# One contraction a chunk from one tile of cosines and sines, waits of the gated unit by quarters, and a written-out sequence per engine

## The chip, the cores and the metric

The kernel runs on one core of one Trainium2 chip. The metric is the device time of one execution in microseconds (us), the median of several runs; less is better. The core has five queues that matter here: TensorE (PE, matrix products), VectorE (DVE), ScalarE (ACT), GpSimd (POOL), and SyncE (SP), which issues the DMA transfers. Each works through its own instructions in the order in which they were written, and an instruction that waits holds up all behind it on that engine.

## The reference

Two branches over a sequence of 2048 positions with 448 channels are mixed by a gate per position:

```python
x = A_u                                             # 1 x 2048 x 448
g = sigmoid((x * gate_w).sum(-1, keepdims=True))
# branch A: a state-space convolution, 256 complex states a channel
dt = exp(log_dt); A = -exp(log_A_real) + 1j * A_imag; C = (C_real + 1j * C_imag) * dt[:, None]
P = exp((A * dt[:, None])[:, :, None] * arange(2048)[None, None, :])
K = 2.0 * einsum("dn,dnl->dl", C, P).real           # a filter of 2048 taps a channel
y = irfft(rfft(u_t, 4096) * rfft(K, 4096))[:, :, :2048]   # causal convolution
a = transpose(y) + u * D_skip
# branch B: a gated linear unit, 448 -> 1792 -> 448
b = einsum("bsf,fd->bsd", sigmoid(x @ w_gate) * (x @ w_up), w_down)
return g * a + (1 - g) * b
```

## The kernel before

All products are made to float32 accuracy. For the large ones each factor is split into a rounded part and a remainder (`wh` and `wl`, `vh` and `vl`, `hh` and `hl` are such pairs; `xs` holds both parts of the input), and three products replace one.

There are four streams of work.

- **Prologue** (tiles of the pools `pre` and `pro`): the gate's dot products (`gt`, `dots`, which give the scales `gs` and `og`), then in two groups of channels the parameters of the filter. Its results go through DRAM as `phd` (phases) and `bsd` (decay steps).
- **Filter** (`kgen`, pools `eg` and `egp`): 28 chunks of 16 channels, each in two half-chunks of 128 states. POOL makes a table of decay powers `tb` from `bs` (one load serves two chunks). In `turns`, PE multiplies phases `ph` by positions into `tp` (L1128); ACT rounds that twice (L1138, L1139, into `fr` and `nn`); PE subtracts the rounded part (L1141); ACT takes the absolute value into `ec` (L1143) and the sine into `fr` (L1144), and turns `ec` into cosines (L1158). DVE multiplies tables into decays `es` (L1165, two products), forms the mirrored half (L1179, L1181), and multiplies `ec` and `fr` by the decays (L1183, L1185). PE contracts over the states into `kp` (L1191): 32 small products a half-chunk, in quarters of its array. ACT copies `kp` into `ke`, and after 14 chunks `ke` goes to DRAM as `kd`, one half of the channels.
- **Convolution** (`Chain`): a transform in two stages (L716, then L749) with a transposition between them, which for one half goes through the DRAM tensor `shf`. Spectra of the input are stored in DRAM as `us`. Later the filter's spectrum is made from `kd`, multiplied (L783), brought back (L793, L830) and added to the output. One large tile `fx_fu` holds in turn the input's first half, its second half, and the filter's first half; `fx_fk` takes the filter's second half in space that the filter's tiles leave.
- **Gated unit**: for each group of two or three blocks of 128 hidden channels, `glu_mm` (L1296 to L1301) gives `gu`, ACT and DVE form the hidden values (L1284 to L1288), `glu_down` (L1313 to L1315) gives `dn`, and L1322 or L1329 adds it to `ob`. Raw weights arrive in the tiles `xr` (five) and `vr` (one), and are split by L1270 and L1272.

The order of instructions is set before the program runs. Each operation is recorded with what it reads and writes and with a cost. `Plan.order` then plays the program through with a clock of those costs: it takes the engine that can start first, and on it the operation of the lowest rank among those that are ready. The table `RANK` gives ranks by engine, tile name and stage. Wherever such a clock lets a DMA's issue cost SP time, it is 450 ns.

Of the kernel before, what the change touches and what calls it, by code (L numbers as in the profile page):

```python
# [415 lines left out]
class Plan:  # L416
# [40 lines left out]
    def order(self):  # L457
# [5 lines left out]
        for key, x in RANK.items():  # L463
            x = x if isinstance(x, tuple) else (x,)
            for j, o in enumerate(kinds[key]):
                o["prio"] = x[j * len(x) // len(kinds[key])]
# [976 lines left out]
```

## Time and profile before

| | us |
|---|---|
| median of 3 runs (lowest to highest) | 741.96 (739.8 to 743.25) |
| the profiled execution, its own time | 740.59 |
| its span, first to last instruction | 738.8 |
| PE busy | 688.4 (93%) |
| DVE busy | 637.9 (86%) |
| ACT busy | 523.7 (71%) |
| POOL busy | 232.7 (32%) |
| mean granted clock of PE | 0.979 |

Busy time counts overlapped instructions once. A matrix product of 512 columns is shown for about 0.39 us though the next one starts 0.23 us after it, so a busy PE can hide lost time. The profile names a tile with its pool: `es_eg` is the tile `es` of the pool `eg`. What is late is read from the waits and from the stretches of time in which engines are less than full.

### The profile page before, as it was taken

Reading aid. Unit: us, or ns where it says so; the run is one execution under the profiler, and the core shown is the slowest. Engines: PE = TensorE matmul, PEld = TensorE weight load, DVE = VectorE, ACT = ScalarE, POOL = GpSimd, SP = SyncE. Lnnn points to the kernel's source line nnn. Section 1 sums busy time; section 2 is a strip of 40 time slices with the busy share of each in tenths; the row PEclk is TensorE's granted clock in tenths of the full one; section 3 lists DMA queues with packets and bytes.
Section 4 is the critical chain, followed back from the end, with each engine's and each line's share of the span. In section 5 each row is a group of like instructions: output and inputs, shape, how many; then the busy total and the mean of one; then the engine's idle time right before and its main releaser. Section 6 shows DMA issues by size and latency. Waiting matters only on the chain.

```text
span 738.8 us, 16536 instructions
## 1 busy us (share of the span) xinstructions
PE 688.4 (93%) x6628; PEld 498.6 (67%) x6628; DVE 637.9 (86%) x847; ACT 523.7 (71%) x962; POOL 232.7 (32%) x282
## 2 busy tenths in 40 slices
PE   4999899999999999978998899999999899999996
PEld 3788777677757776745666677777778566445863
DVE  6999998999999979999898779999995259775976
ACT  5578749999899779998998789999882342233110
POOL 0043446563455435434543324654400000000000
PEclk9999999999999999988999899999999999999998
DMA  9658337925949945469797913239516963787975
GB/s 291 200 122 217 108 79 203 239 91 171 202 121 223 219 107 160 171 175 204 183 232 180 220 45 125 86 133 175 119 40 131 271 226 100 249 304 207 168 191 142
DMA packets 98660, 126.12 MB, mean 171 GB/s; under 512 B 31224, under 2 KB 81080, under 8 KB 97560
## 3 DMA queue, kind: packets, MB, share of 16 engines
q1 hardware_dynamic: 98328, 124.61, 65.0%
q8 instruction: 52, 0.85, 0.5%
q0 software_dynamic: 256, 0.46, 0.3%
q14 instruction: 24, 0.20, 0.1%
HBM read 81.46 MB, written 43.58 MB: 169 GB/s over the span
## 4 chain that ended last, share of the span: by engine, by line
PE 42%; DVE 19%; ACT 16%; DMA 14%; issue 5%; SPq 3%; POOL 2%; ACTq 0%; DVEq 0%
PE kp_egp L1191 4%; PE gu_gps L1296 4%; PE dn_gps L1313 4%; PE gu_gps L1297 4%; PE gu_gps L1298 4%; PE dn_gps L1314 3%; PE dn_gps L1315 3%; DMA fx_fu<-shf 3%; SPq L615 3%; DVE es_eg L1165 2%; PE tp_egp L1128 2%; PE tp_egp L1141 2%; ACT nn_eg L1139 2%; DMA us<-fx_fu 2%; PE fps_fups L716 2%
## 5 line engine op out<-in xcount | busy, mean ns | idle before, releaser
L1296 PE MATMUL gu_gps<-xs_glu,wh_glu 128*128 128x512 f32 x336 | 138.1, 411 | 16.5 <-ACT wh_glu L1270 10.1
L1298 PE MATMUL gu_gps<-xs_glu,wl_glu 128*128 128x512 f32 x336 | 133.2, 397 | 0.4 <-DVE wl_glu L1272 0.4
L1297 PE MATMUL gu_gps<-xs_glu,wh_glu 128*128 128x512 f32 x336 | 133.3, 397 | 0.0
L1165 DVE TENSOR_TENSOR es_eg<-tb_eg 128x1024 f32<-128x1024 f32 x112 | 107.4, 988 | 7.0 <-POOL tb_eg L1115 3.7
L1313 PE MATMUL dn_gps<-vh_glu,hh_glu 128*128 128x448 f32 x224 | 87.9, 393 | 2.8 <-DVE ob_glu L1329 2.6
L1296 PEld LDWEIGHTS gu_gps<-xs_glu,wh_glu 128*128 128x128 f32 x336 | 64.1, 191 | 39.2 <-ACT wh_glu L1270 10.1
L1115 POOL TENSOR_TENSOR tb_eg<-tb_eg 128x96 f32<-128x96 f32 (+2 forms) x84 | 82.2, 982 | 6.2
L1314 PE MATMUL dn_gps<-vh_glu,hl_glu 128*128 128x448 f32 x224 | 82.6, 369 | 0.6 <-issue 0.4
L1315 PE MATMUL dn_gps<-vl_glu,hh_glu 128*128 128x448 f32 x224 | 82.3, 368 | 0.0
L1139 ACT ACTIVATE nn_eg<-fr_eg 128x512 fp32r<-128x512 f32 x112 | 75.0, 669 | 10.3 <-PE tp_egp L1141 10.1
L1329 DVE SCALAR_TENSOR_TENSOR ob_glu<-dn_gps,og,ob_glu 128x448 f32<-128x448 f32 x72 | 48.7, 677 | 30.2 <-PE dn_gps L1315 30.0
L1298 PEld LDWEIGHTS gu_gps<-xs_glu,wl_glu 128*128 128x128 f32 x336 | 64.0, 191 | 15.6 <-DVE wl_glu L1272 1.1
L1297 PEld LDWEIGHTS gu_gps<-xs_glu,wh_glu 128*128 128x128 f32 x336 | 64.2, 191 | 11.4
L1105 POOL MEMSET tb_eg<- 128x96 f32 x28 | 7.8, 283 | 201.1 <-DVE es_eg L1165 200.9
L1144 ACT ACTIVATE fr_eg<-tp_egp 128x512 f32<-128x512 f32 x112 | 69.9, 629 | 0.3 <-PE tp_egp L1141 0.3
L1185 DVE TENSOR_TENSOR es_eg<-fr_eg,es_eg 128x1024 f32<-128x1024 f32 x56 | 69.8, 1246 | 0.1
L1143 ACT ACTIVATE ec_eg<-tp_egp 128x512 f32<-128x512 f32 x112 | 69.4, 625 | 0.3 <-PE tp_egp L1141 0.2
L1183 DVE TENSOR_TENSOR ec_eg<-ec_eg,es_eg 128x1024 f32<-128x1024 f32 x56 | 69.5, 1241 | 0.1
L1138 ACT ACTIVATE fr_eg<-tp_egp 128x512 f32<-128x512 f32 x112 | 64.0, 636 | 7.2 <-DVE es_eg L1185 5.1
L1158 ACT ACTIVATE ec_eg<-ec_eg,half_pi 128x1024 f32<-128x1024 f32 x56 | 67.1, 1197 | 0.1
L1118 POOL TENSOR_TENSOR tb_eg<-tb_eg,bs_eg 128x32 f32<-128x32 f32 x84 | 62.0, 741 | 6.2
L1284 ACT ACTIVATE sg_glu<-gu_gps 128x512 f32<-128x512 f32 x56 | 34.0, 608 | 37.5 <-PE gu_gps L1301 35.3
(154 smaller groups left out, 1423.0 us busy)
## 6 DMA issues: line engine op xcount, KB each, us to landing
shf<-fx_fu SPq DMA_DIRECT2D x16, 896.0 KB, 4.1
fx_fu<-shf SPq DMA_DIRECT2D x16, 896.0 KB, 15.9
us<-fx_fu SPq DMA_DIRECT2D x16, 896.0 KB, 6.7
xr_glu<-in_w_dram SPq DMA_DIRECT2D x52, 256.0 KB, 3.0
ua_fk<-us SPq DMA_DIRECT2D x16, 448.0 KB, 6.0
uax_fk<-us SPq DMA_DIRECT2D x16, 448.0 KB, 4.5
vr_glu<-in_w_dram SPq DMA_DIRECT2D x28, 224.0 KB, 5.1
gt_pre<-in_u_dram SPq DMA_DIRECT2D x8, 448.0 KB, 4.9
```

What stands on the lines that cost most here:

```text
L1115: pool(96 * m, lambda n=n, m=m: G.tensor_mul(g3(n + 1, m), g3(1, m), g3(n, 1).to_broadcast([128, 32, 3, m])))
L1139: op("Act", c_act(512), lambda: S.activation(nn.real, fi(), AF.Copy, scale=-1.0, bias=MAGIC), [(fr, i)], [nn], prio)
L1144: op("Act", c_act(512, True), lambda: S.activation(fr[:, ds], tv(), AF.Sin, scale=TWO_PI), [tp], [(fr, i)], prio, table="sin")
L1165: V.tensor_mul(o.rearrange("p d (i k) -> p d i k", k=ny), x.unsqueeze(3).to_broadcast([128, 16, nx, ny]), y.unsqueeze(2).to_broadcast([128 ...
L1183: op("DVE", c_dve(1024), lambda: V.tensor_mul(ec[:, :, 32:96], ec[:, :, 32:96], es[:, :, 32:96]), [(es, 1), (es, 2)], [(ec, "p")], prio)
L1185: op("DVE", c_dve(1024), lambda: V.tensor_mul(es[:, :, 32:96], fr.real, es[:, :, 32:96]), [fr], [(es, 1), (es, 2)], prio)
L1296: T.matmul(p.real, wh[:, k, cs], x[:, k], start=(k == 0), stop=False)
L1297: T.matmul(p.real, wh[:, k, cs], x[:, 4 + k], start=False, stop=False)
L1298: T.matmul(p.real, wl[:, k, cs], x[:, k], start=False, stop=False)
L1313: T.matmul(p[:, :D], hh[:, ts], vh.real, start=(i == 0), stop=False)
L1314: T.matmul(p[:, :D], hl[:, ts], vh.real, start=False, stop=False)
L1315: T.matmul(p[:, :D], hh[:, ts], vl.real, start=False, stop=(i == len(fs) - 1))
```

## The change

1. **One tile, one contraction.** The tiles `ec` and `fr` become one tile `cs`, with cosines in `cs[:, 0]` and sines in `cs[:, 1]` (three buffers, where `ec`, `fr` and `es` had two each). The two products of 1024 elements by the decays become one of 2048, in place, and the sine's mirrored half is written to `cs` too. So PE reads only `cs`, and `es`, which now stays on DVE, needs one buffer. PE contracts both half-chunks at once: 64 products in a row a chunk instead of twice 32.
2. **Waits by quarters.** A piece of `glu_mm` is recorded as reading the quarter of `x`, `wh` and `wl` that it uses, not all of them.
3. **A fixed sequence.** `RANK` goes. A table `PLACE` gives every operation its place on its engine, and `Plan.order` follows it; its clock only interleaves the engines. In that clock a DMA's issue has its own time (400 ns, or 600 to 3000 ns for transfers of many short pieces) and POOL's operations 85 ns more.
4. **Buffers and loads.** `bs` has one buffer instead of two; `ph` is loaded for one chunk, not two; `sg` has two buffers instead of three; `vr` takes its turn among the `xr` tiles, of which there are four instead of five. The constants `idn` and `pos` were loaded and rounded by two DMAs of POOL; now SP loads them and ACT rounds them (`rounded`, three operations).

```diff
-    ('DVE', 'es', 20): (-560.5, -700, -613.5, -700, -577.5, -249, -611.5, -666.5),
+PLACE = {
+    ('Act', 'ai', 10): (33,),
...
-WB, ECB, FRB, TPB, KPB, GUB, FPS, SGB, XRB = 3, 2, 2, 2, 1, 2, 2, 3, 5
+WB, CSB, PHB, BSB, TPB, KPB, GUB, FPS, SGB, XRB = 3, 3, 2, 1, 2, 1, 2, 2, 2, 4
...
-            self.free[e] = t + (self.ISSUE if e == "SP" else self.CAST)
+            self.free[e] = t + (o["issue"] if e == "SP" else self.CAST)
...
-            o = min((o for t, o in ok if t <= te), key=rank)
-            cand[e].remove(o)
+            te, e = best
+            o = queue[e].pop()
...
-        op("Act", c_act(512, True), lambda: S.activation(fr[:, ds], tv(), AF.Sin, scale=TWO_PI), [tp], [(fr, i)], prio,
-           table="sin")
+        op("Act", c_act(512, True), lambda: S.activation(cs[:, 1, ds, 32:96], block(tp), AF.Sin, scale=TWO_PI),
+           [tp], [(cs, ("s", i))], prio, table="sin")
...
-        op("DVE", c_dve(1024), lambda: V.tensor_mul(ec[:, :, 32:96], ec[:, :, 32:96], es[:, :, 32:96]),
-           [(es, 1), (es, 2)], [(ec, "p")], prio)
-        op("DVE", c_dve(1024), lambda: V.tensor_mul(es[:, :, 32:96], fr.real, es[:, :, 32:96]),
-           [fr], [(es, 1), (es, 2)], prio)
+        op("DVE", c_dve(2048), lambda: V.tensor_mul(
+            cs[:, :, :, 32:96], cs[:, :, :, 32:96], es[:, :, 32:96].unsqueeze(1).to_broadcast([128, 2, 16, 64])),
+           [(es, 1), (es, 2)], cos + sin, prio)
+        return cs
+
+    def contract(parts, kp, prio):
+
         def g():
-            for e in (ec, es):
-                for q in range(4):
-                    for j in range(4):
-                        T.matmul(kp[32 * j:32 * j + 32, q], e[:, 4 * j + q, 64:96], e[:, 4 * j + q, 0:64],
-                                 start=nh == 0 and e is ec and q == 0,
-                                 stop=nh == 1 and e is es and q == 3)
-        op("PE", c_mm4(64, 32, QUARTERS), g, [ec, es], [kp], prio)
+            for cs in parts:
+                for z in range(2):
+                    for q in range(4):
+                        for j in range(4):
+                            T.matmul(kp[32 * j:32 * j + 32, q], cs[:, z, 4 * j + q, 64:96], cs[:, z, 4 * j + q, 0:64],
+                                     start=cs is parts[0] and z == 0 and q == 0,
+                                     stop=cs is parts[1] and z == 1 and q == 3)
+        op("PE", c_mm4(64, 64, QUARTERS), g, parts, [kp], prio)
...
-        vr = glu.tile("vr", 1, (128, D))
-        dma(lambda: vr.real, lambda: w2[128 * f:128 * f + 128], 128 * D * 4, [], [vr], prio)
+        vr = raw_tile(H == 0 and f < 2)
+        vw = lambda: vr.v("p a b -> p (a b)")[:, :D]
+        dma(vw, lambda: w2[128 * f:128 * f + 128], 128 * D * 4, [], [vr], prio)
...
-            op("PE", c_mm(512, 3 if k < 3 else 2), lambda k=k: g(k), [x, wh, wl], [p], pe)
+            z = 2 * (k // 2)
+            op("PE", c_mm(512, 3 if k < 3 else 2), lambda k=k: g(k), [(x, (0, z)), (x, (1, z)), (wh, z), (wl, z)], [p], pe)
...
+    def rounded(t, src, p, n, a=0):
+        xr = raw_tile(True)
+        flat = lambda: xr[:p].rearrange("p a b -> p (a b)")[:, :n]
+        dma(flat, lambda: src[:, a:a + n], p * n * 4, [], [xr], P_PRO)
+        op("Act", c_act(n), lambda: S.activation(t[:, a:a + n], flat(), AF.Copy), [xr], [(t, a)], P_PRO)
...
-    cast(lambda: idn.real, lambda: idt, 128 * 512, [], [idn], 1, 250.0)
-    cast(lambda: pos.real, lambda: post, 96 * 4096, [], [pos], P_PRO)
```

What the new sequence moves is seen at three places. In these lists a row is one instruction: line, operation, what it writes, what it reads, and the size of what it writes; a number behind a name tells buffers apart, and `x4` is four in a row.

PE at a contraction, in the middle of the filter. Before, the second half-chunk of one chunk:

```order
L716 MATMUL fps_fups_1695<-fx_fu_1321,ft_fu_1660 128x224
L716 MATMUL fps_fups_1696<-fx_fu_1321,ft_fu_1660 128x224
L1128 MATMUL tp_egp_1703<-pos_sb,ph_eg_1113 128x512
L1191 MATMUL kp_egp_1626<-ec_eg_1582 32x64 x16
L1191 MATMUL kp_egp_1626<-es_eg_1570 32x64 x16
L1313 MATMUL dn_gps_1744<-vh_glu_1171,hh_glu_1178 128x448
```

Now, both half-chunks of one chunk:

```order
L807 MATMUL fps_fups_1921<-fx_fu_1500,ft_fu_1848 128x224
L807 MATMUL fps_fups_1922<-fx_fu_1500,ft_fu_1848 128x224
L1271 MATMUL kp_egp_1931<-cs_eg_1633 32x64 x32
L1271 MATMUL kp_egp_1931<-cs_eg_1797 32x64 x32
L1392 MATMUL dn_gps_1908<-vh_glu_1338,hh_glu_1818 128x448
```

The contraction stands once a chunk, with 64 products behind each other, and here directly behind first-stage products, which also use a part of the array.

DVE where the first half-chunk begins. Before:

```order
L1049 TENSOR_TENSOR bsx_pro_1265<-th_pro_1135,ex_pro_1132 128x2x7x32
L1272 TENSOR_TENSOR wl_glu_1274<-xr_glu_804,wh_glu_1218 128x512
L1272 TENSOR_TENSOR wl_glu_1274<-xr_glu_841,wh_glu_1218 128x512
L1272 TENSOR_TENSOR vl_glu_1291<-vr_glu_1191,vh_glu_1249 128x448
L1165 TENSOR_TENSOR es_eg_1300<-tb_eg_1162 128x16x64
L1165 TENSOR_TENSOR es_eg_1300<-tb_eg_1162 128x16x32
L1285 SCALAR_TENSOR_TENSOR sg_glu_1253<-sg_glu_1253,gu_gps_1256 128x512
```

Now:

```order
L1363 SCALAR_TENSOR_TENSOR sg_glu_1014<-sg_glu_1014,gu_gps_993 128x512
L1140 TENSOR_TENSOR bsx_pro_1089<-th_pro_779,ex_pro_792 128x2x7x32
L1240 TENSOR_TENSOR es_eg_1097<-tb_eg_940 128x16x64
L1240 TENSOR_TENSOR es_eg_1097<-tb_eg_940 128x16x32
L1254 TENSOR_TENSOR cs_eg_971<-cs_eg_971,es_eg_1097 128x16x32
L1256 SCALAR_TENSOR_TENSOR cs_eg_971<-cs_eg_971,es_eg_1097 128x16x32
L1408 SCALAR_TENSOR_TENSOR ob_glu_651<-dn_gps_1078,og,ob_glu_651 128x448
L1259 TENSOR_TENSOR cs_eg_971<-cs_eg_971,es_eg_1097 128x32x64
L1050 TENSOR_TENSOR lo_pro_1145<-acr_pro_711,hi_pro_1139 112x512
```

The filter's first work on DVE stands ahead of the last of the prologue (`lo`, of the second group of channels), where before the prologue was done by then; and the two products of 1024 are one, of 32 times 64 elements.

SP between the input's first spectrum, written to `us`, and the load of the input's second half into the same tile. Before:

```order
L615 DMA ph_eg_2742<-phd 96x1x256 x2
L615 DMA us_58<-fx_fu_1321 32x2x3584 x4
L615 DMA xr_glu_2901<-in_ut_dram 128x2x256
L615 DMA xr_glu_2914<-in_ut_dram 128x2x256
L615 DMA bs_eg_2939<-bsd 128x320
L615 DMA fx_fu_2980<-in_u_dram 64x4x224 x8
```

Now:

```order
L708 DMA ph_eg_3069<-phd 96x1x256
L708 DMA us_58<-fx_fu_1500 32x2x3584 x4
L708 DMA bs_eg_3263<-bsd 128x320
L708 DMA ph_eg_3269<-phd 96x1x256
L708 DMA skip<-in_dskip_dram 1x2x56
L708 DMA xr_glu_3280<-in_w_dram 128x448
L708 DMA xr_glu_3289<-in_ut_dram 128x2x256
L708 DMA fx_fu_3292<-in_u_dram 64x4x224
L708 DMA xr_glu_3303<-in_ut_dram 128x2x256
L708 DMA xr_glu_3334<-in_ut_dram 128x2x256
L708 DMA fx_fu_3292<-in_u_dram 64x4x224 x2
```

The eight pieces of the load no longer stand together: loads for the gated unit stand between them, and the load of `bs` stands right behind the four large writes.

More of the change, by code (lines that the diff above doesn't have):

```diff
@@ new lines @@
+PLACE = {
+    ('Act', 'aci', 10): (14, 45,),
+    ('Act', 'aci', 19): (73, 100,),
+    ('Act', 'acr', 10): (16, 43, 56,),
+    ('Act', 'acr', 19): (75, 97, 115,),
[26 rows of a table added]
+    ('Act', 'dots', 1): (34,),
+    ('Act', 'dots', 2): (49,),
+    ('Act', 'dots', 16): (79, 93,),
[18 rows of a table added]
+    ('Act', 'idn', 10): (19,),
+    ('Act', 'junk', 10): (39, 68,),
+    ('Act', 'junk', 19): (88, 94, 128,),
[12 rows of a table added]
+    ('Act', 'pos_sb', 10): (91, 61,),
[24 rows of a table added]
+    ('DVE', 'aci', 10): (49,),
+    ('DVE', 'aci', 19): (118,),
+    ('DVE', 'acr', 10): (93,),
+    ('DVE', 'acr', 19): (165,),
[17 rows of a table added]
+    ('DVE', 'dtp', 10): (31,),
+    ('DVE', 'dtv', 10): (27,),
[14 rows of a table added]
+    ('DVE', 'half_pi', 0): (1,),
[22 rows of a table added]
+    ('DVE', 'ones', 10): (3,),
[7 rows of a table added]
+    ('DVE', 'skip', 20): (6,),
[6 rows of a table added]
+    ('DVE', 'uax', 40): (627, 626, 637, 636, 652, 649, 661, 660, 670, 669, 673, 674, 679, 678, 682, 684, 714, 715,
[143 rows of a table added]
@@ L347 @@
 class Clock:
-    ISSUE, CAST, FLIGHT = 450.0, 600.0, 8
+    CAST, FLIGHT = 600.0, 8
     WINDOW, IDLE = 3413.0, 1400.0
@@ L462, in order @@
             kinds.setdefault(o["key"], []).append(o)
[L463 to L466, printed above, removed]
+        for key, places in PLACE.items():
+            for o, place in zip(kinds[key], places, strict=True):
+                o["place"] = place
         outs, need, ready = [[] for _ in ops], [], [0.0] * len(ops)
@@ L474, in order @@
         clock = Clock(engines)
-        cand = {e: [o for o in ops if o["eng"] == e and need[o["i"]] == 0] for e in engines}
+        queue = {e: sorted((o for o in ops if o["eng"] == e), key=lambda o: -o["place"]) for e in engines}
         users, done, left, end, slots = {}, {}, {}, {}, {}
@@ L502, in order @@
             for e in engines:
-                lo, ok = None, []
-                for o in cand[e]:
-                    t = start_of(o)
-                    if t is not None:
-                        ok.append((t, o))
-                        lo = t if lo is None else min(lo, t)
-                if lo is None:
-                    continue
-                te = clock.when(e, lo)
-                if best is None or te < best[0]:
-                    best = (te, e, ok)
+                t = start_of(queue[e][-1]) if queue[e] else None
+                if t is not None:
+                    te = clock.when(e, t)
+                    if best is None or te < best[0]:
+                        best = (te, e)
             if best is None:
                 raise RuntimeError("no instruction can start")
-            te, e, ok = best
-            def rank(o):
-                change = e == "PE" and clock.mode is not None and o["cost"][0][0] != clock.mode
-                return o["prio"] + (CHANGE if change else 0.0), o["i"]
-            o = min((o for t, o in ok if t <= te), key=rank)
-            cand[e].remove(o)
+            te, e = best
+            o = queue[e].pop()
             fin = clock.run(o, te)
@@ L698, in stage1 @@
                     dma(lambda ls=ls, z=z: x[64 * z:64 * z + 64, ls], lambda ls=ls: ap()[:, ls], 64 * 4 * HD * 4, src,
-                        [(x, (z, r)) for r in range(4 * q, 4 * q + 4)], prio, HALF)
+                        [(x, (z, r)) for r in range(4 * q, 4 * q + 4)], prio, HALF, 700.0)
             for q in range(4):
@@ L1151, in half_chunk @@
+        op("Act", c_act(512, True), lambda: S.activation(cs[:, 1, ds, 32:96], block(tp), AF.Sin, scale=TWO_PI),
+           [tp], [(cs, ("s", i))], prio, table="sin")
+    def half_chunk(c, nh, ph, tb, prio):
+        cs = eg.tile("cs", CSB, (128, 2, 16, 96))
+        es = eg.tile("es", 1, (128, 16, 96))
         for i in range(2):
             tp = egp.tile("tp", TPB, (128, 512))
-            turns(c, nh, i, ph, fr, tp, ec, on_pe, prio)
-        if not on_pe:
-            op("Act", c_act(1024), lambda: S.activation(ec[:, :, 32:96], fr.real, AF.Abs), [fr], [ec], prio)
-            op("Act", c_act(1024), lambda: S.activation(fr.real, fr.real, AF.Sin, scale=-TWO_PI), [], [fr], prio,
-               table="sin")
+            turns(c, nh, i, ph, cs, tp, prio)
+        cos, sin = [(cs, ("c", i)) for i in range(2)], [(cs, ("s", i)) for i in range(2)]
@@ L1210, in kgen @@
         kp = egp.tile("kp", KPB, (128, 4, 64))
-        for nh in range(2):
-            half_chunk(c, nh, ph, tb, kp, prio)
+        contract([half_chunk(c, nh, ph, tb, prio) for nh in range(2)], kp, prio)
         def ev():
@@ L1371, in gated_mix @@
     gate(1, 2)
+    rounded(idn, idt, 128, 128)
     sizes = step_sizes(P_PRO)
@@ L1376, in gated_mix @@
     params(1, sizes, P_PRO1)
+    for i in range(2):
+        rounded(pos, post, 96, 512, 512 * i)
     kgen_consts(P_E)
```

135 lines of the change are left out of this document (35 added, 100 removed), and 444 rows, old and new, of tables (PLACE, RANK).

## The prediction

> **What bounds the kernel now.** I read the page first, then a table of stretches, cut where the first and the last contraction of the filter end (142.4 and 556.2) and at the dips between.
>
> ```profile
> span 738.8 us, 16536 instructions
> core 0: us, PE busy (x) PEld busy (x) DVE busy (x) ACT busy (x) POOL busy (x), PEclk, DMA share, GB/s
> 0.00:142.40 142.40, 126.15 (x677) 101.82 (x677) 129.62 (x231) 102.17 (x183) 52.28 (x57) 1.00 0.67 179
> 142.40:234.00 91.60, 89.88 (x1139) 63.61 (x1140) 88.43 (x106) 87.25 (x165) 44.63 (x54) 1.00 0.67 167
> 234.00:262.00 28.00, 24.83 (x284) 19.02 (x282) 25.40 (x29) 20.21 (x37) 13.43 (x18) 0.97 0.93 211
> 262.00:415.00 153.00, 140.17 (x1787) 99.18 (x1787) 143.25 (x173) 142.00 (x264) 65.91 (x86) 0.95 0.72 178
> 415.00:428.00 13.00, 10.21 (x92) 7.38 (x91) 8.55 (x9) 7.39 (x14) 3.58 (x5) 0.74 0.82 171
> 428.00:556.20 128.20, 126.17 (x1643) 96.18 (x1631) 123.05 (x148) 117.92 (x216) 52.92 (x63) 1.00 0.39 103
> 556.20:738.80 182.60, 170.99 (x1032) 111.41 (x1029) 119.66 (x155) 46.74 (x89) 0.00 (x0) 0.98 0.73 201
> ```
>
> Three stages follow. Up to 142.4 the prologue runs and the filter has not delivered. From 142.4 to 556.2 (413.8 us) DVE is busy for 388.7 us and idle for 25.1, ACT and PE are nearly as full: DVE paces, and any of the three that stops soon stops the others. After 556.2 the filter is done and only PE is full: 171.0 of 182.6 us. So what counts is when the filter starts, DVE's work and idle time in the middle, and PE's work at the end.
>
> The waits of PE over the span, and of DVE between 141 and 555, say what makes the idle time; columns are total, times, longest.
>
> ```profile
> PE tp_egp L1141 <- ACT nn_eg L1139: 8.3, 10, 1.9
> PE fps_fkps L716 <- DMA fx_fk<-kd: 3.3, 1, 3.3
> PE fps_fups L716 <- DMA fx_fu<-kd: 2.8, 2, 2.5
> DVE ec_eg L1179 <- ACT ec_eg L1158: 9.8, 7, 4.1
> DVE ob_glu L1329 <- PE dn_gps L1315: 4.1, 2, 3.2
> ```
>
> DVE waits for cosines that come late through PE and ACT (9.8) and for PE's sums (4.1), and PE is held where a transform's first stage waits for its load. The chain of waits around 240 shows such a load:
>
> ```profile
> 238.03 16.29 DMA us<-fx_fu
> 255.13 5.15 DMA fx_fu<-in_u_dram
> 260.32 1.72 PE fps_fups L716 x6
> ```
>
> The tile must be written out (16.3 us) before it is loaded (5.2 us), while PE's sequence goes on to the product that needs it.
>
> **The first stage.** A chunk's first work on DVE needs memory of the prologue's tiles, whose last user is `og`:
>
> ```profile
> 108.38 0.72 DVE L861 TENSOR_SCALAR og<-dots_pre 128x4 f32<-128x4 f32 x1
> 110.81 0.93 SPq L615 DMA_DIRECT2D bs_eg<-bsd  x2
> 114.58 2.79 POOL L1108 TENSOR_SCALAR tb_eg<-bs_eg 128x96 f32<-128x96 f32 x2 [4.90 <-DMA bs_eg<-bsd]
> 123.13 0.69 DVE L1272 TENSOR_TENSOR vl_glu<-vr_glu,vh_glu 128x448 fp32r<-128x448 f32 x1
> 123.75 1.29 DVE L1165 TENSOR_TENSOR es_eg<-tb_eg 128x1024 f32<-128x1024 f32 x1
> L1272 DVE TENSOR_TENSOR wl_glu<-xr_glu,wh_glu 128x512 fp32r<-128x512 f32 x52 | 37.9, 749 | 0.0
> L1285 DVE SCALAR_TENSOR_TENSOR sg_glu<-sg_glu,gu_gps 128x512 f32<-128x512 f32 x56 | 38.0, 679 | 9.6 <-PE gu_gps L1301 7.7 <-ACT sg_glu L1284 1.3 <-ACT hh_glu L1287 0.4
> ```
>
> In the new sequence 19 fewer DVE instructions stand ahead of the end of the first chunk: five remainders of weights (0.749 each), four `sg` (0.679), and ten others (two `hl`, two `es`, six of the prologue's second group) that I put at 0.7. That is 13.5 us; successive instructions overlap by 0.07 (123.13 + 0.69 against 123.75), so 12.3 us of DVE's time. `og` itself stands as far ahead. POOL's table and the loads move with it, and DVE was busy for 129.6 of 142.4 us, so I take all of it: the stage ends at 130.1. The unknown is whether loads and POOL follow; the ends are 0 and 12.3. The constants' move to SP and ACT costs ACT three rounding passes, and the interleaved prologue two more table loads (1.28 us each by the row below); ACT, busy for 102 of 142 us, hides them. Losing POOL's two DMAs frees transfer time at the start; I count nothing.
>
> ```profile
> 0.74 1.28 ACT L1244 ACT_TABLE_LOAD   x1 [0.74 <-PEq L1433]
> ```
>
> **The middle.** The merged product has no row. Its nearest are 512 and 1024 elements (least, median, greatest ns):
>
> ```profile
> L1179 DVE TENSOR_TENSOR ec_eg<-ec_eg,es_eg x56: 673/692/1398, 128.7 to 549.9; 128x512 f32<-128x512 f32 x56
> L1183 DVE TENSOR_TENSOR ec_eg<-ec_eg,es_eg x56: 1204/1216/1524, 130.6 to 551.7; 128x1024 f32<-128x1024 f32 x56
> ```
>
> 512 elements more cost 524 ns, so 2048 cost 2264. Two products less their overlap cost 2 x 1216 - 70 = 2362, so 0.098 is saved, less if the repeated `es` reads slower: 56 times between 0 and 0.098, and I take 0.09, 5.0 us. By the sequence DVE has eight instructions of the gated unit fewer ahead of the last chunk's end (three `vl`, two `wl`, two `sg`, one `ob`: 8 x 0.67 - 0.6 = 4.8 us). The middle thus gets 12.3 from the first stage and gives up 4.8 and 5.0: 388.7 + 2.5 = 391.2 us of DVE.
>
> Its idle time is the large unknown. The dips first: 4.45 us at 415 to 428, where the input's second spectrum and the filter's first half meet. PE's sequence had 1.5 chunks between them and now has two; at 413.8 / 27 = 15.3 us a chunk that is 7.7 us more cover for a wait of 2.5. That dip goes. At the other load (234 to 262, 2.6 idle) it was two chunks and is two: it stays. Of the 9.75 us idle from 262 to 415, at a clock of 0.95, I take half, since PE changes the split of its array less often (below) and recovers faster; and 3.2 of the 8.3 at both ends. Idle comes to 12.5. The ends: none at all, or 25.1 and some 9 more, because the two products of a `tp` stand closer now (by PE's intervals 2.8 us of other work between them in the middle case, before 4.4), and pairs with under 2 us rise from four to nine, each worth up to the longest wait, 1.9. I take 12.5, nearer the row that shows a cause than either end: 403.7 us.
>
> PE's side:
>
> ```profile
> 498.23 0.36 PE L1314 MATMUL dn_gps<-vh_glu,hl_glu 128*128 128x448 f32 x1
> 498.43 0.37 PE L1315 MATMUL dn_gps<-vl_glu,hh_glu 128*128 128x448 f32 x1
> 498.73 0.65 PE L1191 MATMUL kp_egp<-ec_eg 128*32 128x64 f32 x32
> 499.20 0.63 PE L1191 MATMUL kp_egp<-es_eg 128*32 128x64 f32 x32
> 499.76 0.47 PE L1313 MATMUL dn_gps<-vh_glu,hh_glu 128*128 128x448 f32 x1
> 500.07 0.36 PE L1314 MATMUL dn_gps<-vh_glu,hl_glu 128*128 128x448 f32 x1
> 496.67 0.39 PE L1297 MATMUL gu_gps<-xs_glu,wh_glu 128*128 128x512 f32 x1
> 496.89 0.39 PE L1298 MATMUL gu_gps<-xs_glu,wl_glu 128*128 128x512 f32 x1
> ```
>
> Entering the contraction costs 0.30 instead of 0.20, leaving it 0.09 and then 0.31 instead of 0.20: about 0.15 a change of split. I count 259 changes in the old sequence, 182 in the new: 77 x 0.15 = 11.5 us of PE, 62 of them before the last contraction, where DVE paces: there it buys slack, no time. The quarters buy nothing by themselves, as the first product of the run shows:
>
> ```profile
> 9.40 1.28 ACT L1270 ACTIVATE wh_glu<-xr_pre 128x512 fp32r<-128x512 f32 x2
> 10.08 0.80 PE L1296 MATMUL gu_gps<-xs_glu,wh_glu 128*128 128x512 f32 x1 [10.08 <-ACT wh_glu L1270]
> ```
>
> It starts when the first of the two halves of `wh` is rounded, not at 10.68 when both are. The engine already waits by parts; the edit only lets the sequence differ.
>
> **The end.** Ahead of the last contraction stand 39 fewer products of `gu` at 0.22 to 0.23 us (496.67 to 496.89), so PE's end grows by 9.0; 14 fewer changes take off 1.7 to 2.1. The load of `fx_fk` had 63 products of `gu` and 45 of `dn` to hide behind, 63 x 0.23 + 45 x 0.20 = 23.5 us, and has 91 and 36, 28.1: the 3.3 us wait goes, and with it a half-clock spell, 1.7 (half of the 2% of 182.6 that the clock shows missing; the rest is after PE's last work). 182.6 + 9.0 - 1.7 - 5.0 = 184.9.
>
> By the Trainium skill ("TensorE: Matmul & The Clock Gate", Part 1) the clock falls only after an idle window of about 3.4 us. The trace disagrees: 0.74 from 415 to 428, where the longest wait is 2.5. By that rule the 1.7 would not come back, and the sum would be 722.2.
>
> **Sum.** 130.1 + 403.7 + 184.9 = 718.7 of span, and 740.59 - 738.8 = 1.8 around it: 720.5 against the execution's 740.59. The median of the runs is 1.4 above that execution. I say 721.
>
> **Rivals.**
>
> *Only the counts move.* Idle time stays at 25.1 and the `fx_fk` wait remains: 130.1 + 416.3 + 189.9 + 1.8 = 738.1, 0.3% under before, no change. For it: three engines run at 91 to 94% in the middle, and new close pairs replace old waits.
>
> *The sequence fits.* Idle falls to 3 and the end loses its other waits, some 2 us: 130.1 + 394.2 + 182.9 + 1.8 = 709.0. For it: the causes are waits for known transfers. Against: close pairs leave no slack.
>
> *Slower: the single `bs`.*
>
> ```profile
> POOL tb_eg L1105 <- DVE es_eg L1165: 200.9, 26, 12.4
> DMA to landing us min/median/max: 3.7/7.6/11.4
> ```
>
> POOL idles 200.9 / 26 = 7.7 us a chunk before it may overwrite a table. With one `bs` the load can only be issued when POOL has read the old one, so POOL has 7.7 us of idle time and as much slack behind it, 15.4, for it to land. A median landing of 7.6 fits. But SP holds it, and all behind it, until POOL is done, and the new sequence has it right behind four writes of `us` (16.3 us). If that makes it 16.3 + 7.6 at three places, each costs 8.5 us of DVE: 720.5 + 25.5 = 746. It decides from 15.4 us between POOL's last read and landing.
>
> **Chances.** 0.58 for 712 to 732 around 721; 0.18 for the fitting sequence, 700 to 712; 0.15 for counts only, 732 to 741, of which 0.04 still more than 0.5% faster; 0.09 slower than 0.5%. A change under 0.5% is about what a measurement of this kernel can't tell from none, so faster is under 738.3. That makes 0.80 faster, 0.11 same, 0.09 slower. The range, 702 to 740, leaves out the best of the fitting cases and the slow one.
>
> **What would show it.** First contraction ended near 130, last near 534; DVE idle between them 8 to 17 us; no wait of PE for `fx_fk<-kd`; one PE group of 128 `kp` instructions a chunk; the merged product near 2.26 us median. I am wrong if the filter starts no earlier, if POOL waits for `bs_eg`, or if PE's waits for `nn` grow well above 8.3.

## The result, and the profile after

The changed kernel takes 713.69 us (median; 709.97 to 716.87) against 742.49 in the same comparison: a ratio of 0.9607, 95% interval 0.957 to 0.9645. It is faster, and 7 us faster than the 721 that were forecast. The profiled execution took 715.28 us, its span is 713.5.

The stretches of time, cut again where the first and the last contraction end (columns as in the prediction's table), of the kernel after:

```profile
0.00:122.90 122.90, 106.47 (x574) 84.20 (x574) 113.96 (x209) 95.64 (x172) 47.80 (x53) 1.00 0.57 155
122.90:532.30 409.40, 385.91 (x4992) 292.91 (x4988) 388.49 (x423) 380.59 (x702) 188.87 (x228) 0.98 0.66 168
532.30:713.50 181.20, 175.44 (x1069) 117.85 (x1068) 124.51 (x161) 49.02 (x95) 0.00 (x0) 1.00 0.76 211
```

The first stage went from 142.4 to 122.9, the middle from 413.8 to 409.4, the end from 182.6 to 181.2: 19.5 + 4.4 + 1.4 = 25.3 us of span. Most of the gain is the filter's earlier start. In the middle DVE is still the fullest engine, if barely (388.5 us against PE's 385.9), and its idle time (409.4 - 388.5 = 20.9) is not much less than before (25.1). Its largest wait did not shrink: late cosines held it for 9.8 us before, late sines and cosines hold it for 7.5 + 3.9 = 11.4 now, as the second list below shows.

The waits of PE in the middle (total, times, longest), and below them those of DVE in the same stretch:

```profile
PE tp_egp L1220 <- ACT nn_eg L1217: 6.1, 10, 1.4
PE tp_egp L1211 <- ACT cs_eg L1223: 4.4, 6, 2.6
PE kp_egp L1271 <- issue: 2.9, 2, 2.5
PE tp_egp L1211 <- issue: 2.7, 1, 2.7
PE gu_gps L1376 <- issue: 2.5, 1, 2.5
PE dn_gps L1393 <- issue: 2.2, 1, 2.2
```

```profile
DVE cs_eg L1256 <- ACT cs_eg L1223: 7.5, 6, 3.2
DVE cs_eg L1254 <- ACT cs_eg L1233: 3.9, 10, 0.8
DVE ob_glu L1408 <- PE dn_gps L1394: 2.5, 4, 1.3
```

No wait of PE for a load is left; before there were six kinds, 10.8 us in all. In their place stand four stops of 2.2 to 2.7 us that the profile puts down to "issue": PE waited for nothing that the profile shows. One lies in the middle of a contraction, between two of its small products:

```profile
396.30 1.88 PE L1271 MATMUL kp_egp<-cs_eg 128*32 128x64 f32 x119
400.72 0.33 PE L1271 MATMUL kp_egp<-cs_eg 128*32 128x64 f32 x9 [2.54 <-issue]
```

The merged product, and POOL's wait for the single `bs`:

```profile
L1259 DVE TENSOR_TENSOR cs_eg<-cs_eg,es_eg x56: 2275/2292/2854, 105.3 to 527.5; 128x2048 f32<-128x2048 f32 x56
POOL tb_eg L1191 <- DVE es_eg L1240: 169.3, 25, 14.9
POOL tb_eg L1194 <- DMA bs_eg<-bsd: 18.4, 4, 6.2
```

### The profile page after: what moved, and what is told of

It reads as the page before. It is cut to its first block, busy times and chain, and to the rows that moved or that the text cites. A ratio compares the mean times of both kernels' runs of the same rounds, so it can differ in the third digit from the quotient of the medians.

```text
span 713.5 us, 16497 instructions
## 1 busy us (share of the span) xinstructions
PE 667.8 (94%) x6628; PEld 495.0 (69%) x6628; DVE 627.0 (88%) x791; ACT 525.3 (74%) x967; POOL 236.7 (33%) x280
## 4 chain that ended last, share of the span: by engine, by line
PE 58%; ACT 22%; DVE 10%; issue 5%; DMA 4%; SPq 1%; ACTq 0%; DVEq 0%
PE gu_gps L1374 6%; PE gu_gps L1376 6%; PE gu_gps L1375 6%; PE kp_egp L1271 5%; PE dn_gps L1392 5%; PE dn_gps L1393 4%; PE dn_gps L1394 4%; ACT nn_eg L1217 3%; PE tp_egp L1211 3%; ACT cs_eg L1222 3%; ACT cs_eg L1215 3%; PE tp_egp L1220 3%; PE fps_fups L807 2%; PE fps_fups L840 2%; ACT cs_eg L1233 2%
## 5 line engine op out<-in xcount | busy, mean ns | idle before, releaser
L1374 PE MATMUL gu_gps<-xs_glu,wh_glu 128*128 128x512 f32 x336 | 136.1, 405 | 11.0 <-ACT wh_glu L1348 8.5
L1259 DVE TENSOR_TENSOR cs_eg<-cs_eg,es_eg 128x2048 f32<-128x2048 f32 x56 | 132.4, 2364 | 1.0
L1375 PE MATMUL gu_gps<-xs_glu,wh_glu 128*128 128x512 f32 x336 | 132.6, 395 | 0.0
L1201 POOL TENSOR_TENSOR tb_eg<-tb_eg 128x96 f32<-128x96 f32 (+2 forms) x84 | 89.4, 1068 | 5.9
L1217 ACT ACTIVATE nn_eg<-cs_eg 128x512 fp32r<-128x512 f32 x112 | 74.8, 668 | 9.0 <-PE tp_egp L1220 8.0
L1215 ACT ACTIVATE cs_eg<-tp_egp 128x512 f32<-128x512 f32 x112 | 71.1, 640 | 6.0 <-PE tp_egp L1211 4.2
L1222 ACT ACTIVATE cs_eg<-tp_egp 128x512 f32<-128x512 f32 x112 | 69.9, 635 | 2.2 <-PE tp_egp L1220 2.2
L1223 ACT ACTIVATE cs_eg<-tp_egp 128x512 f32<-128x512 f32 x112 | 70.0, 636 | 2.0 <-PE tp_egp L1220 2.0
L1233 ACT ACTIVATE cs_eg<-cs_eg,half_pi 128x1024 f32<-128x1024 f32 x56 | 67.3, 1201 | 0.3
L1191 POOL MEMSET tb_eg<- 128x96 f32 x28 | 7.8, 283 | 178.0 <-DVE es_eg L1240 169.3
L1365 ACT ACTIVATE hh_glu<-sg_glu 128x512 fp32r<-128x512 f32 x56 | 36.7, 655 | 40.5 <-DVE sg_glu L1363 28.3
L1271 PEld LDWEIGHTS kp_egp<-cs_eg 128*32 128x32 f32 x3584 | 53.1, 112 | 13.3 <-issue 11.3
```

The costliest lines, as they stand in the source:

```text
L1201: pool(96 * m, lambda n=n, m=m: G.tensor_mul(g3(n + 1, m), g3(1, m), g3(n, 1).to_broadcast([128, 32, 3, m])))
L1215: op("Act", c_act(512, True), lambda: S.activation(cs[:, 1, ds, 32:96], block(tp), AF.Copy, bias=MAGIC), [tp], [(cs, ("s", i))], prio)
L1217: op("Act", c_act(512), lambda: S.activation(block(nn), cs[:, 1, ds, 32:96], AF.Copy, scale=-1.0, bias=MAGIC), [(cs, ("s", i))], [nn], prio)
L1222: op("Act", c_act(512, True), lambda: S.activation(cs[:, 0, ds, 32:96], block(tp), AF.Abs), [tp], [(cs, ("c", i))], prio)
L1259: op("DVE", c_dve(2048), lambda: V.tensor_mul(cs[:, :, :, 32:96], cs[:, :, :, 32:96], es[:, :, 32:96].unsqueeze(1).to_broadcast([128, 2, 1 ...
L1374: T.matmul(p.real, wh[:, k, cs], x[:, k], start=(k == 0), stop=False)
```

## The experiments

Each run but `ranks` changes the changed kernel in one respect; `ranks` starts from the kernel before. In the table, the first contraction's end, the middle and the end stage are of the one profiled execution of each. Line numbers differ by a few from run to run.

How far such stages vary by themselves is seen where a run does not touch them. The middles of `after` and the three delays take 408.8 to 411.5 us, and the end stage takes 181.1 to 182.2 us in all ten runs that leave it alone.

| run | median us | ratio to before (95%) | first contraction ends | middle | end |
|---|---|---|---|---|---|
| after | 713.69 | 0.9607 (0.957 to 0.9645) | 122.9 | 409.4 | 181.2 |
| delay_start | 730.97 | 0.9842 (0.981 to 0.9874) | 137.8 | 408.8 | 181.1 |
| delay_end | 727.73 | 0.9797 (0.9756 to 0.9837) | 123.7 | 410.0 | 193.5 |
| delay_late | 718.96 | 0.9663 (0.9633 to 0.9692) | 123.8 | 411.5 | 184.6 |
| split_product | 718.03 | 0.9649 (0.9609 to 0.9689) | 123.1 | 411.9 | 181.3 |
| split_contract | 744.13 | 1.0012 (0.9987 to 1.0036) | 124.3 | 439.0 | 181.2 |
| split_ke | 732.17 | 0.986 (0.9827 to 0.9893) | 123.6 | 425.2 | 181.1 |
| early_ke | 717.38 | 0.9652 (0.9623 to 0.9681) | 122.5 | 412.6 | 181.6 |
| early_stage1 | 723.0 | 0.9708 (0.9683 to 0.9733) | 122.8 | 417.3 | 181.1 |
| ranks | 766.19 | 1.0307 (1.0266 to 1.0347) | 143.6 | 430.1 | 185.1 |
| shift_160 | 717.98 | 0.9673 (0.9637 to 0.9708) | 129.4 | 404.6 | 182.2 |
| shift_224 | 718.34 | 0.9672 (0.9637 to 0.9707) | 132.2 | 404.2 | 181.2 |
| lead_24 | 716.25 | 0.9629 (0.9599 to 0.9659) | 123.2 | 405.5 | 181.7 |

### Does the filter's start set the end?

**delay_start**

```diff
+    ('DVE', 'dly', 77): tuple(142 + 0.02 * k for k in range(19)),
...
+    dly = pre.tile("dly", 1, (128, D))
+    op("DVE", c_dve(D), lambda: V.memset(dly.real, 1.0), [], [dly], 77)
+    for _ in range(18):
+        op("DVE", c_dve(D), lambda: V.tensor_mul(dly.real, dly.real, dly.real), [], [dly], 77)
```

> 19 instructions of DVE of 128x448 on a scratch tile, some 10 us, are put just ahead of og, the last step that holds the filter's memory: DVE gets back about the work that the change took from ahead of the filter. Nothing else differs. Theory A: the filter's start passes to the end: first contraction done near 133 instead of 122.9, last near 542, and the time grows by 8.5 to 10.5, to 722 to 724. Theory B: the rest of the program has slack that absorbs it (at the end PE's products of the gated unit fill the time in any case): at most 4 us more, under 718.

Its first two stretches, and PE's longest wait:

```profile
0.00:137.80 137.80, 109.83 (x574) 86.81 (x574) 124.63 (x229) 96.02 (x172) 45.65 (x53) 0.95 0.52 138
137.80:546.60 408.80, 385.69 (x4990) 291.89 (x4988) 389.10 (x423) 381.00 (x702) 200.64 (x228) 0.98 0.67 168
```

```profile
PE gu_gps L1375 <- ACT sg_glu L1363: 13.5, 2, 12.7
```

The first contraction ended 14.9 us later, the span grew by 14.2 (the median by 17.3), and the middle and the end kept their lengths. So a delay of the start passes to the end in full, as theory A has it. Its size was missed by both: DVE got 10.7 us of work, but the gated unit's steps queued behind it, PE waited 12.7 us for them, and its clock fell to a mean of 0.95 in that stretch.

**delay_end** and **delay_late**: the same 19 instructions in the last stage, in a scratch tile of `fk`; the places of `delay_late` are 654.5 + 5 k.

```diff
+    ('DVE', 'dly', 77): tuple(610.5 + 5 * k for k in range(19)),
...
+    dly = fk.tile("dly", 1, (128, D))
```

> The 19 instructions of DVE (some 10 us) that delayed the start by 14.9 us and the end by 14.2 us in their first place are now spread over the stage after the last contraction, where DVE is busy for 124.5 of 181.2 us. Theory A (PE sets the end there, DVE has slack): 713 to 716, at most 2 us more than without them. Theory B (any work on DVE costs its time, since PE also waits for DVE's sums): 8 to 10 us more, 721 to 724.

> The 19 instructions of DVE once more in the last stage, now from the second half's products on (from about 610 on), behind the step where the scratch tile's memory is free; in the first try the first of them held DVE for 8.3 us until the filter was written out. Theory A (PE sets the end, DVE is idle for 56.7 of 181.2 us): at most 2 us more, 713 to 716. Theory B (DVE's steps stand between PE's there, so PE waits for them): 5 to 10 us more, 719 to 724.

In `delay_end` the memory of `fk` was not free, and DVE stood still until the filter had been written out, with PE behind it:

```profile
DVE dly_fk L1487 <- DMA kd<-ke_eg: 8.3, 1, 8.3
...
PE dn_gps L1394 <- DVE hl_glu L1367: 7.3, 1, 7.3
```

So its 12.3 us are mainly that wait, and it does not tell the theories apart. `delay_late` has no such wait:

```profile
535.30:719.90 184.60, 177.36 (x1068) 117.67 (x1068) 133.32 (x180) 49.05 (x95) 0.00 (x0) 1.00 0.76 208
```

DVE is busy for 8.8 us more, the stage is 3.4 longer, which is more than it varies by itself. That lies between the theories: some 40% of DVE's added work passes there, against all and more of it at the start. (The median's 5.3 us also hold differences in the middle, 2.1 us in the profiled execution, which the run does not touch.)

### What paces the middle?

**split_product**

```diff
-        op("DVE", c_dve(2048), lambda: V.tensor_mul(
-            cs[:, :, :, 32:96], cs[:, :, :, 32:96], es[:, :, 32:96].unsqueeze(1).to_broadcast([128, 2, 16, 64])),
-           [(es, 1), (es, 2)], cos + sin, prio)
+        def both():
+            for z in range(2):
+                V.tensor_mul(cs[:, z, :, 32:96], cs[:, z, :, 32:96], es[:, :, 32:96])
+        op("DVE", c_dve(2048), both, [(es, 1), (es, 2)], cos + sin, prio)
```

> The merged product of 2048 elements is written as two of 1024 at the same place. Theory A: DVE paces the stretch between the first and the last contraction, so what the split adds to DVE goes into the time: two of 1216 ns less 70 of overlap are 2362 against 2292, 56 times 0.07 to 0.10, so 4 to 6 us, 718 to 720 against 713.7. Theory B: DVE's time hides in waits for other engines (it is idle for 20.9 of 409.4 us there): less than 1.5 us, 713 to 715.

```profile
123.10:535.00 411.90, 389.28 (x4988) 293.92 (x4988) 395.06 (x477) 381.49 (x702) 183.37 (x227) 0.98 0.66 167
```

DVE is busy for 6.6 us more, the middle is 2.5 longer and the median 4.3 higher. The intervals of the two ratios overlap, and 411.9 is hardly beyond the 408.8 to 411.5 of the untouched middles, so how much of the 6.6 us passes is not settled. In this execution some of it went where DVE had waited: its idle time fell from 20.9 to 16.8.

**split_contract**: the contraction in two halves, the first a third of a chunk earlier on PE.

```diff
+            if key == ("PE", "kp", 20):
+                ends = (places[0] - 25, *places)
+                places = [x for n, (a, b) in enumerate(zip(ends, ends[1:]))
+                          for x in (a + (0.8 if n in (3, 7, 8, 23, 27) else 0.66) * (b - a) + 0.3, b)]
...
-        op("PE", c_mm4(64, 64, QUARTERS), g, parts, [kp], prio)
+        for n, cs in enumerate(parts):
+            op("PE", c_mm4(64, 32, QUARTERS), lambda n=n, cs=cs: g(n, cs), [cs], [kp], prio)
```

> The contraction of a chunk is written as two of 64 products, the first half a third of a chunk earlier on PE (a fifth at five chunks), all else as in the changed kernel. Theory A: the four stops of PE of 2.2 to 2.7 us that the trace of the changed kernel charges to nothing (at 188.9, 250.2, 398.2 and 431.3) come from PE running through 256 instructions, one packet of 16 KB of its queue of instructions, in the 2.0 us of the merged contraction, faster than the next packet comes. Split, at most one of the four is left, DVE's idle time in the middle falls from 20.9 us to 10 to 15, and the time to 704 to 711, although PE pays some 56 more changes of its array's split (8 us by 0.15 each), which lie in PE's slack. Theory B: the merged contraction gains by the changes it saves, and the stops are something else: they stay, PE is 8 us busier, and the time is 715 to 722.

```profile
PE kp_egp L1274 <- ACT ke_eg L1295: 16.2, 10, 2.6
...
PE gu_gps L1377 <- issue: 1.5, 1, 1.5
```

The stops without a cause fell from 10.3 to 1.5 us in total, as theory A has it, but the time rose by 30 us, which neither had. There is one tile `kp`: its first half may not be written before ACT has copied the last sum, and ACT starts that copy up to 13.3 us after the contraction in the changed kernel, up to 14.1 in this run. Merging gave ACT that freedom, and the run had taken it away. Hence two more runs.

**split_ke** moves these copies forward as well, to at most 4.8 us after the contraction in its trace; **early_ke** does only that, with the contraction merged (at most 3.5 us).

```diff
-    ('Act', 'ke', 20): (166, 181, 228, 249, 265, 300, 331, 364, 383, 395, 441, 452, 482, 499, 542, 549, 574, 603, 631,
-        669, 688, 711, 758, 771, 808, 827, 852, 855,),
+    ('Act', 'ke', 20): (154.5, 181, 209.5, 235.5, 265, 289.5, 315.5, 344.5, 370.5, 395, 426.5, 452, 474.5, 499, ...
```

> The split contraction again, but with ACT's copy of each finished sum (ke) moved to some 3 us after its contraction, so that the first half of the next one does not wait for it: in the run with the split alone PE waited 16.2 us for these copies and the middle grew to 443.4 us. Theory A (PE outruns its packets of instructions in the merged contraction): the wait for ke falls under 4 us, no stop of over 1.5 us without a cause is left, DVE is idle for 10 to 16 us in the middle, and the time is 705 to 712. Theory B (the merged contraction gains by the changes of the split that it saves, 56 of them, and PE is nearly as full as DVE there): 716 to 728, with PE busy for some 8 us more than the 385.9 of the changed kernel.

> Only ACT's copies of the finished sums (ke) are moved, to some 3 us after the contraction instead of up to 13.8; the contraction stays merged. It is the control for the split with early copies (732). Theory A: the fixed sequence has no room for a step off its place: 19 copies of 0.7 us that move ahead of the cosines' steps on ACT make them late for PE and DVE, and this alone costs 8 us or more, 721 to 732. Theory B: the move is harmless, 712 to 716, and the 15 us that the middle lost there belong to the split contraction.

The middle of `split_ke`, then that of `early_ke`:

```profile
123.60:548.80 425.20, 399.65 (x4989) 293.36 (x4988) 389.60 (x423) 383.28 (x704) 181.84 (x227) 0.98 0.64 162
```

```profile
122.50:535.10 412.60, 389.01 (x4988) 294.12 (x4988) 388.82 (x423) 381.92 (x702) 194.57 (x228) 0.98 0.66 167
```

The early copies alone cost 3.2 us of the middle, little more than untouched middles differ among themselves; with them the split costs 12.6 us more, 14.8 in the medians. PE is busy for 10.6 us more, some 0.19 for each of the 56 added changes of its split, while DVE does the same work (389.6 against 388.8) and waits. PE also waits longer for ACT's step `nn`, 12.7 us in the middle against 8.3. In `split_ke` no stop without a cause is left. So theory A was right on the stops and wrong on the time, and theory B nearer on the time (732 is beyond its 728): the 23.5 us for which PE was idle in the middle did not absorb what the split added. That the changes of the array's split alone cost this is not shown: the split also puts every first half at a place that the sequence was not fitted to. What a sequence fitted to the split would win back stays open.

**early_stage1**: one place in the table.

```diff
-    ('PE', 'fps', 40): (646, 655, 677, 685, 699, 708, 722, 724, 793, 858, 864, 869, 884, 896, 901, 907, 909, 916, 920,
+    ('PE', 'fps', 40): (636, 655, 677, 685, 699, 708, 722, 724, 793, 858, 864, 869, 884, 896, 901, 907, 909, 916, 920,
```

> The first products of the transform of the filter's first half stand ten places earlier on PE, some 5.6 us, at about 435.5 instead of 441.1; their load is issued at 432.0 as before. Theory A (the distance between a load and its first product is what took the waits for the loads away): PE waits 3 to 6 us for this load again, DVE follows, and the time is 716 to 720. Theory B (PE has slack there, 23.5 of 409.4 us idle): PE waits, but the time stays at 713 to 715.

```profile
437.40 0.64 PE L807 MATMUL fps_fups<-fx_fu,ft_fu 64*128 64x224 f32 x2 [0.18 <-DMA fx_fu<-kd]
441.09 1.48 PE L807 MATMUL fps_fups<-fx_fu,ft_fu 64*128 64x224 f32 x6 [3.04 <-DMA fx_fu<-kd]
442.50 0.80 PE L1374 MATMUL gu_gps<-xs_glu,wh_glu 128*128 128x512 f32 x1
443.09 0.63 PE L1375 MATMUL gu_gps<-xs_glu,wh_glu 128*128 128x512 f32 x1
...
445.33 0.40 PE L1374 MATMUL gu_gps<-xs_glu,wh_glu 128*128 128x512 f32 x1
```

```profile
DVE cs_eg L1256 <- ACT cs_eg L1223: 7.3, 1, 7.3
```

The wait for the load is back, 3.04 us, and the products behind it take 0.63 us instead of 0.40, half clock, for some 2.5 us. DVE waits 7.3 us for the next sines (L1223), the middle grows by 7.9 and the median by 9.3. Not all of that is this wait's: by the ends of the contractions this trace was 1.7 us behind the changed kernel at the 21st, before the wait, and 7.7 us behind at the 22nd, just after it. Theory A holds in kind, and its times were too low: one wait of 3 us cost 6 where it stands. This is the dip of before at 415 to 428, made again by one place in a list.

### Sequence or structure?

**ranks**

```diff
-PLACE = {
+RANK = {
...
-            te, e = best
+            te, e, ok = best
...
+            o = min((o for t, o in ok if t <= te), key=rank)
```

> The changed kernel's structure (cosines and sines in one tile, merged product and contraction, quarters, buffers, places of the constants) under the ranks and the list scheduling of the kernel before, instead of the fixed sequence. Theory A: the sequence carries the gain: without it the filter starts several us later, its loads and waits fall as they will, and the time is 725 to 745, about that of before (742). Theory B: the structure carries it (38 fewer instructions of DVE ahead, merged product, fewer changes of the split): 712 to 720.

```profile
0.00:143.60 143.60, 119.73 (x603) 94.83 (x603) 118.47 (x217) 100.12 (x175) 48.20 (x55) 0.92 0.53 145
143.60:573.70 430.10, 403.14 (x5025) 303.56 (x5021) 393.50 (x425) 381.72 (x705) 170.63 (x225) 0.97 0.65 159
```

The structure of the changed kernel under the old ranks is slower than the kernel before (ratio 1.0307), though DVE has less to do. The filter starts 20.7 us later than in the fixed sequence, and in the middle PE is busy for 17.2 us more and DVE idle for 36.6. The rival, that the structure by itself carries the gain, has fallen, and 766 lies even beyond theory A. The ranks had been fitted to other operations, so the run shows the structure as it is without a fitted order, not the best that ranks could do. How the gain is shared among the quarters, the buffers and the places of the loads within the sequence was not tried.

### The stops without a cause

The page counts the DMA packets of a queue named "instruction" (here `q8`), and PE's products and weight loads:

```profile
PE 667.8 (94%) x6628; PEld 495.0 (69%) x6628; DVE 627.0 (88%) x791; ACT 525.3 (74%) x967; POOL 236.7 (33%) x280
...
q8 instruction: 52, 0.85, 0.5%
```

0.85 MB in 52 packets are 16 KB each. The trace has 13,430 instructions of PE (the 13,256 above and 174 that only wait or signal), 258 for each packet. Counted over all of these, PE had started 2753, 4289, 7873 and 8641 instructions when it stopped at 188.9, 250.2, 398.2 and 431.3: each a multiple of 256 plus 193. Each time a packet of that queue started within 0.5 us of the stop (188.87, 250.09, 398.37, 431.84), and PE went on 2.2 to 2.6 us after the packet's start. I read this as PE running out of instructions, since a contraction is 256 of them in 2.0 us. Shifting PE's program tests it.

**shift_160**, **shift_224** and **lead_24** put 80, 112 and 24 small products ahead; the diff is that of the first.

```diff
+    ('PE', 'fps', 77): (-1,),
...
+    lead = fups.tile("fps", FPS, (128, 512))
+    op("PE", c_mm4(80), lambda: [T.matmul(lead[0:32, 0:4], sizes[3][:, 0:32], sizes[3][:, 0:4], start=True, stop=True)
+                                 for _ in range(80)], [sizes[3]], [lead], 77)
```

> 112 products of 32x4 (with their weight loads 224 instructions of PE) stand ahead of PE's first product, in the 8.5 us in which it waits for the first weights; they write a scratch tile. All else as in the changed kernel, but the limits between packets of 256 instructions now fall elsewhere in PE's program. Theory A (a stop comes where 258 instructions run before the next packet arrives, so where a packet holds mainly a contraction): worked out from the times of the changed kernel, only two places in the middle are left where 258 instructions run in under 4 us (at about 365 and 396), before there were four stops; at most two stops remain, at these places, DVE is idle for 12 to 17 us in the middle, and the time is 707 to 712. Theory B (the stops come with the bursts of transfers, whatever the instruction): the four stops stay at 189, 250, 398 and 431, within 2 us, and the time stays at 713 to 716.

> As the run with 112 small products ahead, but with 80 of them, 160 instructions of PE. Theory A: with this shift eight places in the middle hold 258 instructions in under 3.4 us (at about 139, 168, 202, 230, 262, 293, 473 and 502): five to eight stops there, and the time is 717 to 724. Theory B (the bursts of transfers): four stops as in the changed kernel, 713 to 716.

> 24 small products ahead of PE's first one. The traces of the runs with 80 and 112 show that each is two products and two weight loads, so these were 320 and 448 instructions, 64 and 192 past a whole packet, and that they took 8.7 and 12.1 us and made the start 6.2 and 9.1 us later. 24 of them are 96 instructions and 2.6 us, from 6.0 to 8.6, where PE waits until 8.5. Theory A: the filter starts within 0.5 us of the changed kernel's 122.9; packets end elsewhere, one place where 258 instructions run in under 3 us is left (about 382), there are at most two stops without a cause and the middle takes 404 to 406 instead of 409.4, as in the two other shifts (404.9, 404.4): 707 to 711. Theory B: the middle got shorter there because the start was later (more of the gated unit done ahead of it), not by the shift: 409 again, 713 to 716.

The stops in the middle of `shift_160`, `shift_224` and `lead_24`:

```profile
PE gu_gps L1375 <- issue: 4.7, 1, 4.7
```

```profile
PE kp_egp L1272 <- issue: 3.6, 3, 1.5
PE gu_gps L1375 <- issue: 2.9, 1, 2.9
PE fps_fups L808 <- issue: 0.2, 1, 0.2
```

```profile
PE kp_egp L1272 <- issue: 5.3, 2, 3.9
...
PE dn_gps L1393 <- issue: 0.6, 1, 0.6
...
PE gu_gps L1377 <- issue: 0.2, 1, 0.2
```

With 320 and 448 instructions more the queue has 53 and 54 packets, which fits a queue of PE's own (the pages of `shift_160` and `shift_224`):

```profile
q8 instruction: 53, 0.87, 0.5%
q8 instruction: 54, 0.88, 0.5%
```

The four stops went from their places in all three runs, so they do not belong to the bursts of transfers alone. The largest stop of each came at 7105, 8385 and 6849 instructions, again multiples of 256 plus 193. So where PE runs dry is set by the limits of the packets. But the first two runs shifted by other numbers than I had worked with, as the expectation of the third says, and start 6.5 and 9.3 us later than the changed kernel; their times do not decide between the theories. Where theory A had five to eight stops for `shift_160`, one came.

A limit, the place where a packet ends, that is reached fast is not enough. In the trace of `shift_160` seven limits had the 258 instructions before them run in 2.6 to 4.5 us; one of them, at 356, got a stop of 4.7 us, and six got none of note. In the changed kernel two more such limits, at 9409 and 10177 instructions, had their packet start no later than 0.3 us after PE had come within 258 instructions of them, and no stop of note; at the four stops it was 3.1 to 4.8 us. So the packet must be late too. Over all limits of the changed kernel it started up to 12.5 us after that point. Why a packet is late stays open.

What the stops cost is less clear. The middles of the three shifted runs are 404.2 to 405.5 us, those of the four unshifted runs with an untouched middle 408.8 to 411.5; so some 4 to 5 us. A later start is not the reason: `delay_start` starts later still, and its middle takes 408.8. But `lead_24`, which starts as early as the changed kernel (123.2), has a median of 716.25, just above what theory B had, and the intervals of the two ratios overlap; its profiled execution was the fastest of its six. No gain in time is shown, and it is not offered as a better version.

## Why the prediction was right, and where it was off

The prediction summed 130.1 + 403.7 + 184.9 for the profiled execution, with 1.8 around them, and got 720.5. It measured 122.9 + 409.4 + 181.2 and 715.28: the stages are off by -7.2, +5.7 and -3.7. The time, 713.69, is in the case that was held likeliest, 712 to 732, but near its lower end, and that the sum is off by only 5.2 is partly luck, since the stages' errors cancel. So is the last contraction's end, 532.3 where 534 was named. Two of the named signs did not come as named: the first contraction ended at 122.9 and not near 130, and DVE's idle time of 20.9 us is outside the 8 to 17 and nearer to the rival's 25.1.

**The first stage: right in kind, 7.2 us short.** Up to the first contraction's end DVE works 114.0 us instead of 129.6, so 15.7 less, against my 12.3. The rows count 22 fewer instructions there (209 against 231), I had 19; three at 0.7 and the overlap that I took off (1.2) would make up the gap. The rest is idle time that fell from 12.8 to 8.9, of which I had counted nothing. `delay_start` shows that the start passes to the end, and `ranks`, whose filter starts at 143.6, that the sequence brought it forward.

**The middle: DVE's work about right, its idle time mis-sized.** DVE's work came to 388.5 against the forecast 391.2, its idle time to 20.9 against 12.5. The waits for loads went as named, even the one at 234 to 262 that I had kept, and `early_stage1` shows what such a wait was worth. The feared rise of the waits for `nn` did not come (7.5 against 8.3 over the span). What I did not see is that the merged contraction can leave PE without instructions: 9.9 us of stops in the middle, for which the shifted runs suggest 4 to 5 us. In those runs DVE still idles for 15.7 to 17.2 us, so the stops explain about half of the gap to 12.5; the rest stays open. Their middles of 404.2 to 405.5 are near my 403.7 partly by chance: DVE has less work there than I had.

**"There it buys slack, no time": this step is not borne out.** I counted the 62 fewer changes of PE's split in the middle as slack, since DVE paces. `split_ke` against `early_ke` put 56 of them back, which made PE busier by 10.6 us and the middle longer by 12.6: at least in this sequence, PE's added time was not absorbed. How I explain it, that PE, ACT and DVE pass a chunk to and fro and what delays PE delays DVE, fits the longer waits for `nn`, but the split's unfitted places are a rival that no run takes away.

**The merged product: 2292 ns, forecast 2264.** By medians and my formula (2362 for the two) it saves 0.07 instead of 0.09 each, 3.9 us instead of 5.0. `split_product`, which puts the two products back, makes DVE busier by 6.6 us in the middle; this counts slow single instructions too, which a median leaves out. So the saving is some 4 to 7 us, and the forecast lies between.

**The end: 3.7 us better.** PE's busy time rose by 4.4 (171.0 to 175.4), where I had 9.0 - 1.7 for the changes - 1.7 for the half-clock spell, 5.6. PE's idle time fell from 11.6 to 5.8, by 5.8 where I had 3.3: the end lost its other waits too, as the rival of the fitting sequence had it.

**The rivals.** "Only the counts move" needed the `fx_fk` wait and is out. "Slower: the single `bs`" is out as well: POOL does wait longer for `bs` (18.4 us against 4.9, up to 6.2), which I had named as a sign that I am wrong, but POOL has 169.3 us of other idle time, and DVE waits only 0.5 us for its tables. That sign was badly chosen: the wait that counts was DVE's. That the quarters buy nothing by themselves was not tried.

## What to carry to other kernels

Where three engines are above 90% and hand work to and fro in a fixed order, do not book an engine's idle time as slack: price a step by the wait that it causes on the next engine. Here a wait of 3 us for a load cost 6. Count the instructions ahead of the first step of the longest stream: a delay there passed to the end in full, and of work added in the last stage some 40% did. A better structure without an order fitted to it can be slower than the old kernel, so the two are to be priced together.
